# Output gates and a SiLU computed from tanh in a fused mLSTM, SiLU and Mish kernel

## The chip, the cores and the metric

One Trainium2 chip, one of its cores. The metric is device time in microseconds of one execution of the whole program; lower is better. Three runs of the kernel before took 449.8 to 451.85 us, with a median of 450.71 us.

## What is computed

Three stages in float32, each fed by the one before. Batch 2, 8 heads, 768 positions, head dimension 40; the two feed-forward layers have a model width of 320 and a hidden width of 2048, on 1536 tokens.

```python
# attention (mLSTM), per position t
m_new = max(f + m, i);  f_stab = exp(f + m - m_new);  i_stab = exp(i - m_new)
C = f_stab * C + i_stab * outer(v, k);  n = f_stab * n + i_stab * k
y = sigmoid(o_gate) * (C @ q) / max(abs(n @ q), 1)
# layer one
h = x @ w_in;   g = h * sigmoid(h);            x = g @ w_out
# layer two
h = x @ w_in2;  g = h * tanh(softplus(h));     out = g @ w_out2
```

## The kernel before

**Tiles and stages.** The 768 positions are cut into six chunks of 128. The attention of a chunk is done in its parallel form: TensorE makes the scores (L748), ScalarE the decay weights as exponentials (L704 for the first two chunks, L730 for the others), VectorE multiplies them (L757, the tile `pt`), TensorE sums (L762), and the state carried from chunk to chunk is updated by L846, L853, L860 and L866. The output of a chunk is divided and gated (L805 to L819), where the tile `y` holds the output gate, and turned (L897, L907, L910) into `xh` and `xl`. The gate's sigmoid is line L649, once for each chunk, in place, on 128x640 elements.

**The feed-forward layers.** A float32 matrix product is made of three passes on split operands: a rounded high part and the remainder. The weights of a layer come as 16 tiles of 128x704. Each is loaded by a DMA into one of three `wr` buffers, put together by ScalarE (L471, L463) and VectorE (L477), and split into `wh` (ScalarE, L503; VectorE, L501) and `wl` (GpSimd, L497). Hidden units are processed in pairs of 128. For a pair, `gemm1` (L930) writes the PSUM tile `h`, an activation makes `g`, `parts` splits that into `gh` (GpSimd, L955) and `gl` (VectorE, L957), and `gemm2` (L947 to L949) adds to the PSUM tiles `o`. Layer one has 48 such pairs (8 pairs of units for each of 6 chunks), layer two as many. `gemm2` of a pair is issued two pairs behind its `gemm1`. PSUM holds two tiles `h`; `g` has two buffers. In layer one the activation is ScalarE's SiLU (L964); layer two uses ScalarE's Mish function (L973, L974).

**The first two chunks of layer one** are done in two halves: units 0 to 4 first and 5 to 7 later, since the weights are still coming. The first part's result is stored by L983 (ScalarE) and the second added by L987 (VectorE), both from PSUM into the tile `y`.

**ScalarE's tables.** A function of ScalarE is served from a table that must be loaded. In the kernel before, the exponential, the sigmoid, the SiLU and the Mish function are marked with four different tables ("exp", "sig", "silu", "mish"). A change of table is an instruction ACT_TABLE_LOAD ahead of the function; the profile gives it the function's line.

**The order of the work.** Nothing runs in the order in which it is written. Each piece is registered with an engine, a cost in us, its tiles and for some its table. A planner in the kernel then simulates the engines, and in its model a change of table costs 1.28 us and adds a penalty of 20 to an operation that needs one. It draws 1,500 random variations of the priorities from a fixed seed, and keeps the best order. This order is fixed when the program is built; each engine then works through its own list, and an instruction that waits holds up those behind it. Transfers are all issued by SyncE's queue.

Of the kernel before, what the change touches and what calls it, by code (L numbers as in the profile page):

```python
# [13 lines left out]
AF = mybir.ActivationFunctionType  # L14
ALU = mybir.AluOpType
# [23 lines left out]
class Plan:  # L39
# [13 lines left out]
    def buf(self, pool, shape, dtype, tag, bufs=1, name=None):  # L53
        b = Buf(pool, shape, dtype, tag, bufs, name or tag)
        ring = self.rings.setdefault((id(pool), tag), [])
        b.before = ring[-bufs] if len(ring) >= bufs else None
        b.prev = ring[-1] if ring else None
        ring.append(b)
        return b

    def op(self, eng, cost, fn, r=(), w=(), table=None, anchor=None, hurry=0.0, duty=1.0, spare=False, after=(), size=0.0, grain=0.0):
        o = Op()
        o.eng, o.cost, o.fn, o.table, o.anchor, o.hurry = eng, cost, fn, table, anchor, hurry
        o.n, o.duty, o.spare, o.size, o.grain = len(self.ops), duty, spare, size, grain
        deps, order = {}, {}

        def need(ops):
            for d in ops:
                deps[d.n] = d

        for write, keys in ((False, r), (True, w)):
            for k in keys:
                b, sub = k if isinstance(k, tuple) else (k, None)
                subs = [s for s in dict.fromkeys([*b.wr, *b.rd]) if sub is None or s is None or s == sub]
                for s in subs:
                    need(b.wr.get(s, ()))
                    if write:
                        need(b.rd.get(s, ()))
                if not b.users:
                    if b.before is not None:  # L80
                        need(b.before.users)
                    if b.prev is not None:
                        order[b.prev.users[0].n] = b.prev.users[0]
                else:
                    order[b.users[0].n] = b.users[0]
                b.users.append(o)
        for d in after:
            order[d.n] = d
        for k in r:
            b, sub = k if isinstance(k, tuple) else (k, None)  # L90
            b.rd.setdefault(sub, []).append(o)
        for k in w:
            b, sub = k if isinstance(k, tuple) else (k, None)
            if sub is None:
                b.wr, b.rd = {None: [o]}, {}
            else:
                b.wr[sub], b.rd[sub] = [o], []
        deps.pop(o.n, None)
        order.pop(o.n, None)
        o.deps = list(deps.values())  # L100

        o.order = [d for d in order.values() if d.n not in deps]
        self.ops.append(o)
        return o
# [265 lines left out]
def kernel(  # L370
# [17 lines left out]
    DM = out.shape[1]  # L388
# [10 lines left out]
    op, buf = plan.op, plan.buf  # L399
    pe, act, dve, pool = nc.tensor, nc.scalar, nc.vector, nc.gpsimd  # L400
# [242 lines left out]
    y1 = [buf(sb, [128, B, DM], F32, f"y{c}") for c in range(NCH)]  # L643
# [2 lines left out]
    last = NCH - 1  # L646

    def sigm(c, after):
        return op("ACT", 0.74, lambda: act.activation(out=y1[c].t, in_=y1[c].t, func=AF.Sigmoid),  # L649
           w=[y1[c]], table="sig", after=after)  # L650

    def load_o(c, after=()):
        dma(y1[c], None, lambda: y1[c].t, lambda: og[c], 128 * B * DM * 4, after=after)
# [1 line left out]
    def attention(c):  # L655
# [79 lines left out]
        for i in SIGS.get(c, ()):  # L735
            sigm(i, [last_e[0]])
# [217 lines left out]
    def parts(g, gh, gl):  # L954
        op("POOL", 0.63, lambda: pool.tensor_scalar(  # L955
            out=gh.t, in0=g.t, scalar1=1.0, scalar2=1.0, op0=ALU.mult, op1=ALU.mult), r=[g], w=[gh])
        op("DVE", 0.75, lambda: dve.tensor_tensor(  # L957
            out=gl.t, in0=g.t, in1=gh.t.bitcast(F32), op=ALU.subtract), r=[g, gh], w=[gl], grain=1.0)

    def silu(hp):  # L960
        g = buf(sb, [128, 512], F32, "g", bufs=2)
        gh = buf(sb, [128, 512], F32R, "gh", bufs=3)
        gl = buf(sb, [128, 512], F32R, "gl", bufs=3)
        op("ACT", 0.6, lambda: act.activation(out=g.t, in_=hp.t, func=AF.Silu), r=[hp], w=[g], table="silu")  # L964
        parts(g, gh, gl)
        return gh, gl

# [11 lines left out]
    def store_y(c, b, po, part):  # L979
        y = y1[c]  # L980

        def first():
            act.copy(out=y.t[:, b, :], in_=po.t[:, 0:DM])  # L983


        def more():
            dve.tensor_tensor(out=y.t[:, b, :], in0=y.t[:, b, :], in1=po.t[:, 0:DM], op=ALU.add)  # L987

        if part == 2:
            op("DVE", 0.49, more, r=[po], w=[(y, b)])  # L990
        else:
            op("ACT", 0.43, first, r=[po], w=[(y, b)])
# [21 lines left out]
    def block(l, c, ps_, part=0, lag=2):  # L1014
        po = None
        for p in ps_:
            hp = hidden(l, p)
            for f in range(2):
                gemm1(l, 2 * p + f, xt[l, c], hp)
            g = (silu, mish)[l](hp)  # L1020
            while len(pend) >= lag:
                drain()
            if po is None:
                po = [buf(ps, [128, 512], F32, f"o{b}") for b in range(2)]
            pend.append((l, c, p, g, po, p == ps_[0], p == ps_[-1], part))
# [7 lines left out]
    for c in range(YFIRST):  # L1033
        load_o(c)
    sig = [sigm(c, ()) for c in SIGS.get(-1, ())]
    dma(sel, None, lambda: sel.t, lambda: cst[0:16, NC0:], 16 * 126 * 4)
    if G1 == 0:
# [171 lines left out]
```

## Time and profile before

| | |
|---|---|
| median of three runs | 450.71 us (449.8 to 451.85) |
| span of the profiled execution, first to last instruction | 447.9 us |
| mean granted TensorE clock | 0.973 |
| busy share: TensorE / weight load | 97% / 95% |
| busy share: VectorE / ScalarE / GpSimd | 44% / 56% / 32% |

The whole time of the profiled execution is not listed apart from its span; the median of the runs lies 2.8 us above the span, and covers what lies ahead of the first and behind the last instruction. In the profile PE is TensorE, PEld its weight loads, ACT ScalarE, DVE VectorE, POOL GpSimd and SP SyncE; L964 is line 964 of the kernel. A busy share is a mean over stages that have different limits, so the rows below are taken by stage.

### The profile page before, as it was taken

To read this page: it belongs to the slowest core of one execution; us is meant where nothing else is said; L and a number is where in the kernel's file an instruction comes from. 1 tells how busy PE (TensorE), PEld (TensorE's weight loads), DVE (VectorE), ACT (ScalarE), POOL (GpSimd) and SP (SyncE) were. 2 spreads that over 40 slices of the span, in tenths; PEclk is the share of its full clock that TensorE was granted. 3 is DMA by queue.
4 is the path that set the end of the run, shared out by engine and by line. 5 is a ranking of instruction groups with operands and counts; after the bars stand their busy time and mean duration, and the time that the engine had idled before them with its cause. 6 is when DMAs were issued, how large, how long until landed. Compare 5 with 4: busy or idle time off the path is not lost.

```text
span 447.9 us, 8297 instructions
## 1 busy us (share of the span) xinstructions
PE 435.0 (97%) x3366; PEld 424.6 (95%) x3366; DVE 196.2 (44%) x340; ACT 249.4 (56%) x441; POOL 145.1 (32%) x208
## 2 busy tenths in 40 slices
PE   7978989999999999999999999999999999999997
PEld 4858889999999999999999999999999999999996
DVE  4486587644774555664442644322131221221111
ACT  1898667799989888873124447433343333333331
POOL 1777686862361434122113996300000000000000
PEclk9956969999999999999999999999999999999999
DMA  7869979152475767865000453100000000000000
GB/s 223 301 225 268 324 241 318 67 166 71 112 249 185 291 213 277 279 205 201 3 1 1 131 156 103 34 31 0 2 31 0 1 31 0 31 1 0 31 2 29
DMA packets 16785, 54.18 MB, mean 121 GB/s; under 512 B 2003, under 2 KB 3731, under 8 KB 16267
## 3 DMA queue, kind: packets, MB, share of 16 engines
q1 hardware_dynamic: 16747, 53.65, 36.5%
q8 instruction: 26, 0.43, 0.4%
q14 instruction: 12, 0.10, 0.1%
HBM read 45.88 MB, written 7.77 MB: 120 GB/s over the span
## 4 chain that ended last, share of the span: by engine, by line
PE 89%; POOL 4%; ACT 3%; DMA 2%; issue 1%; DVE 1%; POOLq 0%; ACTq 0%
PE h L930 29%; PE o L947 12%; PE o L949 12%; PE o L948 12%; PE s L930 10%; PE a L762 4%; PE s L748 2%; POOL wl L497 2%; PE a L897 2%; DMA wr<-w 2%; PE o L445 1%; PE a L781 1%; PE a L846 1%; ACT e L704 1%; PE h L694 1%
## 5 line engine op out<-in xcount | busy, mean ns | idle before, releaser
L947 PE MATMUL o<-wh,gh 128*128 128x320 f32 x384 | 121.1, 315 | 0.0
L949 PE MATMUL o<-wh,gl 128*128 128x320 f32 x384 | 119.1, 310 | 0.4 <-DVE gl L957 0.4
L948 PE MATMUL o<-wl,gh 128*128 128x320 f32 x384 | 118.4, 308 | 0.0
L930 PE MATMUL h<-xh,wh 128*128 128x256 f32 x432 | 111.0, 286 | 0.0
L930 PE MATMUL h<-xl,wh 128*128 128x256 f32 x432 | 109.0, 281 | 0.0
L975 DVE TENSOR_TENSOR gl<-e,gh 128x512 fp32r<-128x512 f32 x48 | 33.8, 703 | 126.6 <-ACT e L974 126.6
L930 PEld LDWEIGHTS h<-xh,wh 128*128 128x128 f32 x432 | 82.5, 191 | 0.6 <-issue 0.2
L930 PEld LDWEIGHTS h<-xl,wh 128*128 128x128 f32 x432 | 82.3, 190 | 0.0
L949 PEld LDWEIGHTS o<-wh,gl 128*128 128x128 f32 x384 | 72.1, 188 | 0.7 <-DVE gl L957 0.7
L947 PEld LDWEIGHTS o<-wh,gh 128*128 128x128 f32 x384 | 72.3, 188 | 0.5
L948 PEld LDWEIGHTS o<-wl,gh 128*128 128x128 f32 x384 | 72.3, 188 | 0.0
L497 POOL TENSOR_TENSOR wl<-wt,wh 128x192 fp32r<-128x192 f32 x96 | 64.7, 704 | 15.9 <-ACT wh L503 13.4
L957 DVE TENSOR_TENSOR gl<-g,gh 128x512 fp32r<-128x512 f32 x48 | 40.6, 851 | 43.9 <-POOL gh L955 43.7
L930 PE MATMUL h<-xh,wl 128*128 128x256 f32 x288 | 58.0, 283 | 0.0
L955 POOL TENSOR_SCALAR gh<-g 128x512 fp32r<-128x512 f32 x48 | 32.3, 674 | 77.2 <-ACT g L964 74.9
L964 ACT ACTIVATE g<-h 128x512 f32<-128x512 f32 x48 | 28.5, 598 | 41.4 <-PE h L930 40.9
L930 PEld LDWEIGHTS h<-xh,wl 128*128 128x128 f32 x288 | 44.3, 190 | 0.0
L973 ACT ACTIVATE gh<-h 128x512 fp32r<-128x512 f32 x24 | 14.5, 602 | 50.5 <-PE h L930 50.4
L973 ACT ACTIVATE gh<-s 128x512 fp32r<-128x512 f32 x24 | 14.4, 601 | 49.5 <-PE s L930 49.5
L930 PE MATMUL s<-xh,wh 128*128 128x256 f32 x144 | 36.4, 282 | 0.0
L930 PE MATMUL s<-xl,wh 128*128 128x256 f32 x144 | 36.0, 279 | 0.0
L477 DVE SCALAR_TENSOR_TENSOR wt<-wt,wr 128x704 int32<-128x704 int32 x32 | 31.8, 997 | 5.7 <-ACT wt L463 5.1
(101 smaller groups left out, 621.0 us busy)
## 6 DMA issues: line engine op xcount, KB each, us to landing
wr<-w SPq DMA_DIRECT2D x32, 704.0 KB, 6.4
wd<-wt SPq DMA_DIRECT2D x16, 352.0 KB, 5.3
wt<-wd SPq DMA_DIRECT2D x16, 352.0 KB, 3.1
vk<-vk SPq DMA_DIRECT2D x6, 729.0 KB, 4.0
kq<-qk SPq DMA_DIRECT2D x12, 320.0 KB
e<-gd SPq DMA_DIRECT2D x8, 256.0 KB, 5.9
ga<-gd SPq DMA_DIRECT2D x8, 256.0 KB, 3.3
y<-og SPq DMA_DIRECT2D x6, 320.0 KB, 11.3
```

The lines of the kernel that those rows point to most:

```text
L477: dve.scalar_tensor_tensor(out=ti, in0=ti, scalar=3, in1=r.t[:, :, 0], op0=ALU.logical_shift_left, op1=ALU.bitwise_or)
L497: pool.tensor_tensor(out=wl.t[:, k], in0=t.t[:, k], in1=wh.t[:, k].bitcast(F32), op=ALU.subtract)
L762: pe.matmul(out=pa.t[:, h * V:(h + 1) * V], lhsT=pt.t[:, i * 128:(i + 1) * 128], rhs=vb.t[:, b, h * V:(h + 1) * V], start=True, stop=True,)
L930: pe.matmul(out=hp.t[:, f % 2 * 256:(f % 2 + 1) * 256], lhsT=w.t[:, k], rhs=xx.t[:, i, :], start=(n == 0), stop=(n == len(terms) - 1),)
L947: pe.matmul(out=o, lhsT=gh.t[:, ts], rhs=wh.t[:, O], start=(first and f == 0), stop=False)
L948: pe.matmul(out=o, lhsT=gh.t[:, ts], rhs=wl.t[:, O], start=False, stop=False)
L949: pe.matmul(out=o, lhsT=gl.t[:, ts], rhs=wh.t[:, O], start=False, stop=(end and f == 1))
L955: op("POOL", 0.63, lambda: pool.tensor_scalar(out=gh.t, in0=g.t, scalar1=1.0, scalar2=1.0, op0=ALU.mult, op1=ALU.mult), r=[g], w=[gh])
L957: op("DVE", 0.75, lambda: dve.tensor_tensor(out=gl.t, in0=g.t, in1=gh.t.bitcast(F32), op=ALU.subtract), r=[g, gh], w=[gl], grain=1.0)
L964: op("ACT", 0.6, lambda: act.activation(out=g.t, in_=hp.t, func=AF.Silu), r=[hp], w=[g], table="silu")
L973: op("ACT", 0.6, lambda: act.activation(out=gh.t, in_=hp.t, func=AF.Mish), r=[hp], w=[gh], table="mish")
L975: op("DVE", 0.7, lambda: dve.tensor_tensor(out=gl.t, in0=g.t, in1=gh.t.bitcast(F32), op=ALU.subtract), r=[g, gh], w=[gl])
```

## The change

The sigmoid of the output gates becomes `0.5 * tanh(x / 2) + 0.5`: ScalarE makes the tanh in place, GpSimd multiplies and adds in place. Layer one's SiLU becomes `(tanh(h / 2) + 1) * h`, which is twice the SiLU: ScalarE makes the tanh from PSUM, and a new VectorE instruction adds one and multiplies by `h`, again from PSUM. The factor two is taken out where the layer's result leaves PSUM: ScalarE's copy becomes a multiplication by 0.5, and VectorE's addition takes a scalar 0.5 with it. All three functions are now marked with the exponential's table; Mish keeps its own. The planner gets 54 more operations (6 on GpSimd, 48 on VectorE) and other tables, and plans the whole order anew.

```diff
     def sigm(c, after):
-        return op("ACT", 0.74, lambda: act.activation(out=y1[c].t, in_=y1[c].t, func=AF.Sigmoid),
-           w=[y1[c]], table="sig", after=after)
+        o = op("ACT", 0.74, lambda: act.activation(out=y1[c].t, in_=y1[c].t, func=AF.Tanh, scale=0.5),
+           w=[y1[c]], table="exp", after=after)
+        op("POOL", 0.85, lambda: pool.tensor_scalar(
+            out=y1[c].t, in0=y1[c].t, scalar1=0.5, scalar2=0.5, op0=ALU.mult, op1=ALU.add), w=[y1[c]])
+        return o
...
-        op("ACT", 0.6, lambda: act.activation(out=g.t, in_=hp.t, func=AF.Silu), r=[hp], w=[g], table="silu")
+        op("ACT", 0.6, lambda: act.activation(out=g.t, in_=hp.t, func=AF.Tanh, scale=0.5), r=[hp], w=[g], table="exp")
+        op("DVE", 0.7, lambda: dve.scalar_tensor_tensor(
+            out=g.t, in0=g.t, scalar=1.0, in1=hp.t, op0=ALU.add, op1=ALU.mult), r=[hp], w=[g])
         parts(g, gh, gl)
...
         def first():
-            act.copy(out=y.t[:, b, :], in_=po.t[:, 0:DM])
+            act.mul(out=y.t[:, b, :], in_=po.t[:, 0:DM], mul=0.5)
...
         def more():
-            dve.tensor_tensor(out=y.t[:, b, :], in0=y.t[:, b, :], in1=po.t[:, 0:DM], op=ALU.add)
+            dve.scalar_tensor_tensor(
+                out=y.t[:, b, :], in0=po.t[:, 0:DM], scalar=0.5, in1=y.t[:, b, :], op0=ALU.mult, op1=ALU.add
+            )
```

## Rows read from the trace of the kernel before

**Rows 1.** Head of the page.

```profile
span 447.9 us, 8297 instructions
```

**Rows 2.** Windows by stage: length, busy us (instructions) by engine, granted clock, DMA share, GB/s.

```profile
0.00:70.00 70.00, 60.35 (x409) 52.40 (x409) 45.01 (x90) 48.18 (x91) 45.65 (x68) 0.83 0.82 265
...
120.00:130.00 10.00, 10.00 (x91) 9.68 (x90) 8.70 (x13) 8.30 (x12) 6.24 (x7) 1.00 0.62 188
130.00:266.00 136.00, 136.00 (x1101) 134.68 (x1101) 69.49 (x120) 81.41 (x133) 50.99 (x73) 1.00 0.49 167
266.00:448.00 182.00, 178.69 (x1377) 178.37 (x1376) 44.21 (x73) 67.07 (x127) 13.59 (x22) 1.00 0.07 24
```

**Rows 3.** Windows within the first 70 us; engines in order PE, PEld, DVE, ACT, POOL.

```profile
20.00:23.00 3.00, 2.76 (x25) 2.65 (x23) 0.42 (x1) 2.99 (x7) 2.81 (x7) 1.00 0.57 163
23.00:26.00 3.00, 0.77 (x4) 0.77 (x4) 2.31 (x4) 3.00 (x6) 0.53 (x2) 0.66 0.22 33
...
45.00:50.00 5.00, 4.57 (x33) 4.31 (x32) 3.23 (x5) 3.62 (x6) 2.85 (x4) 1.00 1.03 287
...
57.00:62.00 5.00, 5.00 (x36) 4.73 (x35) 4.32 (x9) 2.99 (x5) 4.31 (x6) 0.61 0.70 252
62.00:67.00 5.00, 3.98 (x23) 3.79 (x22) 3.78 (x10) 3.01 (x5) 4.24 (x7) 0.71 0.69 191
```

**Rows 4.** Chain that ended last, 0 to 75 us: start us, us, what.

```profile
17.73 1.28 ACT L649
...
19.77 1.28 ACT L704
...
23.69 0.04 DVE wt L477
...
24.50 0.69 DVE pt L757
...
46.94 0.90 DVE wt L477
...
47.85 7.42 DMA wr<-w
```

**Rows 5.** The same chain later, two pairs of layer one.

```profile
131.99 1.89 PE h L930 x16
135.63 1.89 PE h L930 x16
```

**Rows 6.** ScalarE's timeline near 40 us: start, us, instruction.

```profile
39.63 1.28 ACT L649 ACT_TABLE_LOAD   x1
...
41.68 1.28 ACT L964 ACT_TABLE_LOAD   x1
42.97 0.60 ACT L964 ACTIVATE g<-h 128x512 f32<-128x512 f32 x1
```

**Rows 7.** Groups by line, whole span: busy us, mean ns of one | idle before, releaser.

```profile
L964 ACT ACTIVATE g<-h 128x512 f32<-128x512 f32 x48 | 28.5, 598 | 41.4 <-PE h L930 40.9
...
L964 ACT ACT_TABLE_LOAD x15 | 19.2, 1283 | 3.4 <-PE h L930 3.2
...
L649 ACT ACT_TABLE_LOAD x6 | 7.7, 1283 | 0.1
L957 DVE TENSOR_TENSOR gl<-g,gh 128x512 fp32r<-128x512 f32 x48 | 40.6, 851 | 43.9 <-POOL gh L955 43.7
L757 DVE TENSOR_TENSOR pt<-e,s 128x512 f32<-128x512 f32 x16 | 10.7, 682 | 4.9 <-PE s L748 4.9
L955 POOL TENSOR_SCALAR gh<-g 128x512 fp32r<-128x512 f32 x48 | 32.3, 674 | 77.2 <-ACT g L964 74.9
```

**Rows 8.** Waits of DVE, 70 to 266 us: us in total, times, longest.

```profile
DVE gl L957 <- POOL gh L955: 40.2, 28, 3.6
DVE nm L789 <- PE a L781: 11.6, 6, 3.1
```

**Rows 9.** Waits of SyncE's queue, 0 to 75 us.

```profile
SPq L403 <- DVE wt L477: 28.2, 13, 5.0
```

## The prediction, made before the changed kernel was built or run

> **What bounds the kernel now.** I read the windows first, cut by stage. From 130 us on TensorE is busy in all of the window, 136.00 of 136, at a granted clock of 1.00, and from 266 us to the end it misses only 3.3 us, which is the last store behind the last product [rows 2]. At 120 to 130 us the other engines are at their fullest (DVE 8.70 of 10, ACT 8.30) and TensorE still misses nothing. So behind the first 70 us the kernel is as long as its matrix products, and ScalarE's work and its table loads are no limit there. In the first 70 us it is otherwise: TensorE is idle for 70 - 60.35 = 9.65 us, and its mean granted clock is 0.83, so that part of what it does there goes at the lower of its two levels, 1.2 GHz [rows 2]. Only these 70 us can be made shorter. Removing 20 table loads or 50 from the rest is worth nothing by itself.
>
> Next I read where the holes of the first 70 us lie. From 20 to 26 us TensorE is busy for 2.76 + 0.77 of 6 us, a hole of 2.47 us; DMA falls to a share of 0.22 at the same place, and ScalarE is busy for 5.99 of the 6 us [rows 3]. The chain of waits says why: it runs through ScalarE from 17.73 us, a table load, the sigmoid, a second load to come back to the exponential, exponentials, the two steps of a weight tile, then VectorE's joining of that tile (23.69 us) and only behind it, in VectorE's fixed order, the `pt` that TensorE waits for (24.50 us) [rows 4]. The same joining frees a `wr` buffer, and SyncE's queue waits for such joins for 28.2 us in all [rows 9]; so the weight stream stands still there too. Later there are smaller holes: 0.43 us at 45 to 50 and 1.02 us at 62 to 67 us, with clocks of 0.61 and 0.71 from 57 to 67 us [rows 3].
>
> **The change, part by part.**
>
> *Table loads removed.* With one table for exponentials, gates and SiLU, the 15 loads in front of the SiLU and the 6 in front of the sigmoid go, 19.2 + 7.7 us of ScalarE at 1,283 ns each [rows 7], and so do those by which the exponential comes back. But only four of all of these lie in the first 70 us: two at 17.73 and 19.77 us [rows 4], and two at 39.63 and 41.68 us [rows 6].
>
> The first two are 2.56 us on the chain, with ScalarE full around them. What they delay is the hole of 2.47 us, so TensorE can win between 0 (if `pt`'s buffers or another engine become the last to be ready) and 2.47 us. I take the whole of it, because the chain between the loads and `pt` has nothing in it but ScalarE and one VectorE join, and because the weight stream, which is let go by the same join, moves with it. Term one: -2.47 us.
>
> Of the second two, the load at 41.68 us delays the first SiLU to 42.97 us [rows 6]. That starts the path to the first `gl`, for which TensorE misses 0.43 us [rows 3]. The SiLU gains 1.28 us, or 2.56 with the other load, and loses the new VectorE instruction (below, 0.68 us). The join at 46.94 us, which the chain goes through into a transfer of 7.42 us [rows 4], could come earlier too, but the DMA engines show a share of 1.03 there [rows 3], so an earlier issue only queues. Between 0 and -2.56 us, I take the small hole. Term two: -0.4 us.
>
> How much one switch costs decides both terms. The trace has a load at 41.68 us that takes 1.28 us, and the SiLU behind it starts at 42.97 us, 0.01 us after it ends [rows 6]. The Trainium skill, ScalarE: Activation LUTs, "What ACT_TABLE_LOAD costs", adds a drain of about 1.38 us to the load, 2.66 us for a switch. By that the first two switches would hold up the weight stream by 5.3 us instead of 2.56, and if TensorE followed the stream the forecast would be an estimated 445.0 us. The trace shows no room for such a drain behind the load, so 1.28 us stands.
>
> *The new VectorE instruction* reads `g` and PSUM and writes 128x512 elements, 48 times. The nearest row is `pt`, which has the same shape and also one operand in PSUM: 682 ns; the other end is `gl` with 851 ns while GpSimd works [rows 7]. I take 0.68 us, 48 x 0.68 = 33 us. The first follow the SiLU at 42.97 us [rows 6], where VectorE has room (busy 3.23 of 5 us at 45 to 50) [rows 3]; the rest falls in the stretch where VectorE is about half busy, 69.49 of 136 us [rows 2]. It lies in the path of each pair and also keeps `h` longer. Two pairs follow each other at 135.63 - 131.99 = 3.64 us, of which one pair's `gemm1` is 1.89 [rows 5]. A tile `h` is needed again two pairs later, so 2 x 3.64 - 1.89 = 5.4 us after it is complete. ScalarE's 0.60 and VectorE's 0.68 leave 4.1 us of slack. `gemm2`, two pairs behind, has still more: its path needs 0.60 + 0.68 + 0.67 + 0.85 = 2.8 us against 2 x 3.64 = 7.3 us from the end of its `gemm1` to its turn (two `gemm1` and two `gemm2`). Term three: 0, between 0 and what the rival below gives.
>
> *The new GpSimd instruction*, 128x640, 6 times: `gh` with 512 columns takes 674 ns [rows 7], so 0.84 us by columns, 5.1 us in all. Two gates fall before 70 us [rows 4, 6]. GpSimd works for 45.65 us of these 70 [rows 2], so each could cost from 0 to 0.84 us. But it is busy for only 0.53 of 3 us at 23 to 26 and 2.85 of 5 at 45 to 50 us [rows 3], and the first two chunks' gates leave time to choose. I take 0, with 1.7 us for the range.
>
> *tanh for SiLU and sigmoid, multiply for copy, scalar-tensor-tensor for add*: same engines, shapes and number of instructions. I take 0. The SiLU's 598 ns and the store's time may differ by a few ns, in a stretch that TensorE covers. No DMA is added.
>
> *The order.* The planner draws anew, with 54 more operations and no price on changing between exponentials, gates and SiLU. What it finds in the first 70 us I can't work out. The trace bounds it by the idle 9.65 us on the one side; I allow 2 us either way.
>
> **The sum.** 447.9 [rows 1] - 2.47 - 0.4 = 445.0 us of span. The median of the runs lies 2.8 us above the profiled span, so 447.8 us. About 0.5%, 2.25 us, is what a measurement can tell from no change: faster is below 448.5, slower above 453.0.
>
> **The rivals.**
>
> *The start gets tighter all over (B).* Freed of the switching penalty, exponentials of the third chunk and SiLU can alternate, and feed TensorE in the holes at 57 to 67 us: 1.02 us of idleness and, at clocks of 0.61 and 0.71, 0.39 x 5 + 0.29 x 5 = 3.4 us of lower rate, of which I count half. 447.8 - 1.0 - 1.7 = 445.1 us. For it speaks that both are there to be had; against it, that GpSimd is busy for 4.31 and 4.24 of 5 us there [rows 3] and gains nothing.
>
> *Hidden behind the weight stream (C).* The hole at 20 to 26 us goes, but the weight tiles come no earlier, because the DMA engines are full at 45 to 50 us, and TensorE waits later for the 2.47 us that it won: 447.8 + 2.5 = 450.3 us. For it speaks the share of 1.03 [rows 3]. Against it: the stream stood nearly still at 23 to 26 us (0.22), so time given there isn't lost to a full queue.
>
> *VectorE's list blocks (D), slower.* The new instruction stands in a list in which `nm` and `gl` wait for others for up to 3.1 and 3.6 us [rows 8], and at 120 to 130 us VectorE is busy 8.70 of 10 us. Where such a wait and the work queued behind it exceed the 4.1 us of slack of `h`, TensorE stalls, which it never does now. Eight attention halves lie behind 70 us; a microsecond lost at each is +8, with the gain 447.8 + 8 = 455.8 us. It decides once the stalls exceed 453.0 - 447.8 = 5.2 us in sum. Against it: the planner models VectorE's occupation and these waits, and a single wait stays below the slack.
>
> *The loads don't go (E).* If tanh were served from another table than the exponential, every switch would stay, and only VectorE's and GpSimd's work be added: 451 to 453 us. The trace has no tanh. The Trainium skill, ScalarE: Activation LUTs, "Table sets: the hidden batching unit", lists tanh in the exponential's set; no run here shows it yet.
>
> **How the numbers follow.** The forecast (A) gets 0.46, with a range of its own from 446.3 to 449.3; B 0.15, C 0.21, D 0.15, E 0.03. Faster: 0.38 of A and all of B, 0.53. Same: 0.08 of A, 0.17 of C, 0.02 of E, 0.27. Slower: D, 0.04 of C and 0.01 of E, 0.20. The range reaches 2 us below B for a luckier order, 443, and up to 453.5, which takes in C with both GpSimd terms (450.3 + 1.7) and leaves most of D out.
>
> **What would show it.** Right: only two or three table loads in the whole trace; the chain between 17 and 25 us without L649's load; TensorE's hole at 20 to 26 us gone or below 1 us; the idle time of the first 70 us down from 9.65 to about 7 us; behind it TensorE as full as now, and L964's new VectorE instruction near 0.68 us. Wrong: idle time of TensorE behind 70 us with VectorE as its releaser (D); a new hole between 45 and 70 us as large as the old one (C); or a hole that the new order opened elsewhere in the start.

## The result, and the profile after

The changed kernel takes 455.09 us (median of 4 runs, 452.82 to 458.7) where the kernel before takes 450.25 us on the same chip: a ratio of 1.0119, 95% interval 1.0075 to 1.0164. The forecast was 447.8 us, and the measured time lies above the range. By the prediction's own bound (453.0 us) this is "slower", to which it gave a chance of 0.20.

Head of the page, windows by stage (columns as in [rows 2]) and groups by line of the changed kernel:

```profile
span 454.1 us, 8366 instructions
```

```profile
0.00:70.00 70.00, 57.08 (x372) 47.63 (x373) 48.02 (x87) 38.89 (x80) 42.45 (x64) 0.85 0.77 239
...
120.00:130.00 10.00, 10.00 (x84) 9.47 (x83) 8.59 (x18) 6.75 (x16) 5.40 (x7) 1.00 0.77 243
130.00:266.00 136.00, 136.00 (x1102) 134.69 (x1101) 87.09 (x149) 55.02 (x102) 49.73 (x70) 1.00 0.50 161
```

```profile
L968 DVE SCALAR_TENSOR_TENSOR g<-g,h 128x512 f32<-128x512 f32 x48 | 32.9, 685 | 26.7 <-ACT g L967 26.4
...
L651 POOL TENSOR_SCALAR y<-y 128x640 f32<-128x640 f32 x6 | 4.6, 763 | 9.8 <-ACT y L649 9.8
...
L607 ACT ACT_TABLE_LOAD x1 | 1.3, 1283 | 0.8 <-PEq L1206 0.8
L978 ACT ACT_TABLE_LOAD x1 | 1.3, 1283 | 0.0
```

The span grew by 6.2 us over [rows 1]. Table loads: two are left, one at the start and one before Mish; all others are gone, as the Trainium skill, ScalarE: Activation LUTs, "Table sets: the hidden batching unit", has it with tanh in the exponential's set. The new VectorE instruction takes 685 ns. Behind 70 us TensorE is as full as in [rows 2], though VectorE now works 87.09 of 136 us there instead of 69.49. The visible loss lies in the first 70 us: TensorE is busy for 57.08 us instead of 60.35, so it misses 12.92 us instead of 9.65.

Windows within the start, changed kernel:

```profile
15.00:20.00 5.00, 4.88 (x28) 4.03 (x29) 1.83 (x6) 1.32 (x6) 0.00 (x0) 0.55 0.82 314
20.00:23.00 3.00, 3.00 (x20) 2.72 (x21) 1.15 (x5) 2.14 (x7) 0.55 (x1) 0.61 0.12 35
23.00:26.00 3.00, 3.00 (x33) 2.80 (x30) 0.42 (x1) 1.84 (x8) 1.40 (x2) 1.00 0.32 76
45.00:50.00 5.00, 4.75 (x37) 4.48 (x36) 4.18 (x6) 1.72 (x3) 5.00 (x8) 1.00 0.99 292
57.00:62.00 5.00, 4.71 (x42) 4.59 (x42) 3.96 (x9) 3.38 (x6) 2.57 (x5) 1.00 0.84 249
62.00:67.00 5.00, 2.52 (x21) 2.32 (x21) 4.87 (x7) 2.51 (x5) 5.00 (x8) 0.97 0.89 249
```

One of these windows in the kernel before:

```profile
15.00:20.00 5.00, 5.00 (x49) 4.62 (x49) 3.21 (x7) 4.50 (x12) 3.63 (x3) 1.00 0.82 268
```

Against [rows 3]: the hole at 20 to 26 us is closed (6.00 of 6 us busy). But the clock, which was 1.00 at 15 to 23 us before, is 0.55 and 0.61 there, and at 62 to 67 us TensorE now misses 2.48 us instead of 1.02 (it waits at L849 for VectorE's `nm`, L792). What happens just ahead of the low clock is seen on three engines. VectorE's timeline of the changed kernel (start, us, instruction):

```profile
8.21 1.28 DVE L538 TENSOR_TENSOR_SCAN ga<-ga 80x512 f32<-80x512 f32 x1
9.52 1.39 DVE L576 TENSOR_SCALAR ga<-ga,gc 16x128 f32<-16x128 f32 x1
10.95 1.37 DVE L565 TENSOR_TENSOR ga<-ga 80x128 f32<-80x128 f32 x1
...
13.84 1.22 DVE L576 TENSOR_SCALAR ga<-ga,gc 16x128 f32<-16x128 f32 x1
```

GpSimd's timeline and then TensorE's, same kernel:

```profile
9.57 1.26 POOL L546 TENSOR_TENSOR ga<-ga 80x512 f32<-80x512 f32 x1 [6.90 <-DVE ga L538]
10.91 1.26 POOL L551 TENSOR_TENSOR ga<-ga 80x512 f32<-80x512 f32 x1
...
13.73 1.26 POOL L565 TENSOR_TENSOR ga<-ga 80x512 f32<-80x512 f32 x1
```

```profile
15.12 0.29 PE L600 MATMUL a<-ct,ga 80*128 80x80 f32 x1 [1.67 <-DMA qq<-q]
```

VectorE's timeline of the kernel before, the same stretch:

```profile
7.79 0.29 DVE L565 TENSOR_TENSOR ga<-ga 80x128 f32<-80x128 f32 x1
8.09 0.28 DVE L576 TENSOR_SCALAR ga<-ga,gc 16x128 f32<-16x128 f32 x1
...
9.45 0.28 DVE L576 TENSOR_SCALAR ga<-ga,gc 16x128 f32<-16x128 f32 x1
10.73 1.28 DVE L538 TENSOR_TENSOR_SCAN ga<-ga 80x512 f32<-80x512 f32 x1
```

The gate arithmetic of the first chunks comes in two lots: chunks 0 and 1 (two tiles of 80x128) and chunks 2 to 5 (80x512). Before, the scan over the second lot (L538, 80x512) stood behind the last gate operation of the first. In the new list it stands ahead of the last of them. When it ends, GpSimd starts its own 80x512 operations on the second lot, and three of VectorE's small operations beside them take 1.39, 1.37 and 1.22 us instead of 0.28 or 0.29. Each of the three ends within 0.2 us of the end of the GpSimd instruction beside it. The last one ends at 15.06 us, and TensorE, which needs its `ga` for L600, stands from 13.45 to 15.12 us. (The releaser in brackets, `qq`, is not the one that came last: L600 reads `ga`.) Then the clock falls.

### The profile page after: what moved, and what is told of

It is laid out like the page before. It is cut to its first block, busy times and chain, and to the rows that moved or that the text cites. A ratio compares the mean times of both kernels' runs of the same rounds, so it can differ in the third digit from the quotient of the medians.

```text
span 454.1 us, 8366 instructions
## 1 busy us (share of the span) xinstructions
PE 437.9 (96%) x3366; PEld 425.1 (94%) x3366; DVE 230.8 (51%) x388; ACT 209.1 (46%) x409; POOL 149.7 (33%) x214
## 4 chain that ended last, share of the span: by engine, by line
PE 81%; POOL 6%; DVE 5%; DMA 4%; issue 2%; ACT 1%; SPq 1%; POOLq 0%; ACTq 0%
PE h L933 26%; PE o L950 11%; PE o L952 11%; PE o L951 11%; PE s L933 10%; PE a L765 3%; PE s L751 3%; POOL wl L497 3%; DMA qq<-q 2%; DMA e<-gd 2%; PE a L900 2%; POOL gh L958 1%; PE a L784 1%; PE a L849 1%; DVE wt L477 1%
## 5 line engine op out<-in xcount | busy, mean ns | idle before, releaser
L933 PE MATMUL h<-xl,wh 128*128 128x256 f32 x432 | 110.2, 283 | 0.0
L968 DVE SCALAR_TENSOR_TENSOR g<-g,h 128x512 f32<-128x512 f32 x48 | 32.9, 685 | 26.7 <-ACT g L967 26.4
```

The source lines that it names most:

```text
L933: pe.matmul(out=hp.t[:, f % 2 * 256:(f % 2 + 1) * 256], lhsT=w.t[:, k], rhs=xx.t[:, i, :], start=(n == 0), stop=(n == len(terms) - 1),)
L968: op("DVE", 0.7, lambda: dve.scalar_tensor_tensor(out=g.t, in0=g.t, scalar=1.0, in1=hp.t, op0=ALU.add, op1=ALU.mult), r=[hp], w=[g])
```

## The experiments

A list is the order in which the planner's operations are issued. In the runs on lists the search is left out and a written-out list is used, so that a single instruction can be moved. Each median is compared with the kernel before on the same chip; the ratios can be compared between rows, the medians only within a chip. "Tanh alone" and the two runs with a part of the new instructions (e5, e9, e10, e12) leave out what the output needs and serve to time the rest.

| run | us | ratio (95% interval) |
|---|---|---|
| e1 changed instructions, list of before | 457.53 | 1.0168 (1.0116 to 1.0220) |
| e2 instructions of before, new list | 470.85 | 1.0456 (1.0394 to 1.0517) |
| e5 tanh alone, list of before | 449.56 | 0.9997 (0.9970 to 1.0024) |
| e9 tanh and GpSimd's six, list of before | 449.08 | 0.9987 (0.9967 to 1.0006) |
| e10 tanh and VectorE's 48, list of before | 455.06 | 1.0119 (1.0083 to 1.0154) |
| e6, e7 before, seeds 2 and 4 | 449.02, 450.78 | 0.9998 (0.9969 to 1.0027), 1.0034 (1.0007 to 1.0061) |
| e8, e4 changed, seeds 2 and 3 | 451.11, 450.83 | 1.0035 (1.0015 to 1.0055), 1.0023 (1.0001 to 1.0046) |
| e3 changed, scan moved | 452.61 | 1.0065 (1.0034 to 1.0097) |
| e13 and cut moved | 450.44 | 1.0008 (0.9990 to 1.0025) |
| e14 and gate transfers later | 449.96 | 0.9999 (0.9985 to 1.0013) |
| e17 and tiles placed as before | 448.17 | 0.9969 (0.9952 to 0.9986) |
| e16 before, scan ahead | 451.17 | 1.0035 (1.0013 to 1.0056) |
| e18 before, tiles placed as after | 452.03 | 1.0046 (1.0022 to 1.0069) |
| e11 before, gate transfers later | 448.13 | 0.9966 (0.9938 to 0.9994) |
| e12 tanh alone, gate transfers later | 448.24 | 0.9964 (0.9936 to 0.9993) |
| e15 changed, seed 3, gate transfers later | 450.16 | 1.0020 (1.0001 to 1.0039) |

### List and instructions apart (e1, e2)

```diff
-        for o in best:
-            o.fn()
+        for n in ORDER:      # e1: before's list, the 54 new operations put in where due
+            self.ops[n].fn() # e2: kernel before, the new list without those 54
```

> The changed kernel's instructions in the order that the kernel before runs in; the 54 new instructions are put in where their inputs are due, nothing is planned anew. Theory T (the newly drawn order is slower, the new instructions are not): 446 to 450 us, at or below the kernel before's 450, no table loads but two, and TensorE's idle time in the first 70 us at or below 9.65 us. Rival R (the VectorE and GpSimd instructions themselves cost 5 us, in any order): 453 us or more.

> The kernel before's instructions (sigmoid and SiLU functions, with their table loads) in the order that the changed kernel runs in; the 54 new ones are left out, nothing is planned anew. T: as slow as the changed kernel or slower, 453 to 460 us, since the order carries the loss and the loads come on top. R: about 450 us, since what costs is left out.

Measured: 457.53 and 470.85 us. Neither list carries the other's instructions, and the forecast of e1 that the old list would be 446 to 450 us with them fell; e2 lies above both of its forecasts too. In e2 the trace has 31 table loads, in a list that was drawn without a price on them. In e1 the start keeps its gain: the step that stood at 23.69 us in [rows 4] comes at 22.05 us. But gemm1 of the first pair starts at 38.49 us, as before at 38.38, and behind 70 us, where the planned lists show no hole, TensorE now waits for the new instructions. So e1 had to be taken apart.

### Loads, gate arithmetic and products one at a time (e5, e9, e10)

```diff
-        act.activation(out=y1[c].t, in_=y1[c].t, func=AF.Sigmoid)   # and Silu
+        act.activation(out=y1[c].t, in_=y1[c].t, func=AF.Tanh, scale=0.5)
...
+        pool.tensor_scalar(...)           # e9 alone
+        dve.scalar_tensor_tensor(...)     # e10 alone
```

> The order of the kernel before, tanh in place of sigmoid and SiLU, and none of the 54 new instructions: the output lacks the halving and adding behind the gates and the product behind the tanh. It shows what the table loads alone are worth in that order. Theory T (the loads do hold up the start, by the 2.9 us of the prediction): 446 to 448 us, with the first 70 us idle for 7 us or less. Rival L (the loads were covered by other engines, and their time is lost again at the next wait): 449 to 451 us, like the kernel before.

> The order of the kernel before, tanh in place of sigmoid and SiLU, with the 6 new GpSimd instructions for the gates and without the 48 VectorE products (so layer one's activation is tanh alone). It parts the 7 us that the 54 new instructions cost in that order. Theory V (VectorE's products in a list that was not made for them are what costs): 449 to 451 us. Rival G (GpSimd's six in front of the weight splits): 455 us or more.

> The same order, with the 48 VectorE products and without the 6 GpSimd instructions (so the gates are tanh alone). V: 455 to 458 us, TensorE idle behind 70 us with VectorE's product or what follows it as the releaser. G: 449 to 451 us.

Measured: the missing loads are worth nothing (0.9997), the six GpSimd instructions cost nothing (0.9987), and VectorE's 48 cost about 5.5 us over e5 in a list that was not drawn for them (1.0119 against 0.9997). TensorE's timeline in e10, with what ended its idle time in brackets:

```profile
86.55 0.38 PE L870 MATMUL h<-xh,wh 128*128 128x256 f32 x1 [1.29 <-DVE g L905]
95.64 0.41 PE L887 MATMUL o<-wh,gh 128*128 128x320 f32 x1 [1.54 <-POOL gh L895]
96.75 0.42 PE L889 MATMUL o<-wh,gl 128*128 128x320 f32 x1 [0.55 <-DVE gl L897]
```

This is rival D as it was described: gemm1 waits for a tile `h` that the product (L905) still reads, and gemm2 for the parts of `g`.

Where the gain of the loads goes is read in e5. Its windows, then the same windows of the kernel before:

```profile
20.00:23.00 3.00, 2.71 (x26) 2.59 (x24) 2.10 (x4) 3.00 (x7) 2.92 (x6) 1.00 0.67 171
23.00:26.00 3.00, 2.30 (x24) 2.13 (x25) 2.37 (x5) 3.00 (x9) 3.00 (x4) 1.00 0.97 293
...
54.00:66.00 12.00, 12.00 (x64) 11.70 (x64) 8.23 (x17) 6.34 (x11) 8.63 (x13) 0.50 0.61 204
```

```profile
54.00:66.00 12.00, 11.53 (x79) 10.98 (x77) 8.68 (x18) 7.17 (x12) 10.30 (x16) 0.72 0.76 254
```

The hole at 20 to 26 us shrinks from 2.47 to 0.99 us, the transfers go on through it (share 0.97 instead of 0.22 at 23 to 26 us), and the first gemm1 starts at 36.62 us instead of 38.38. VectorE's join, which stood at 23.69 us in [rows 4], is at 20.91 us:

```profile
20.91 0.89 DVE L416 SCALAR_TENSOR_TENSOR wt<-wt,wr 128x704 int32<-128x704 int32 x1 [0.90 <-ACT wt L402]
```

Then, in the chain of waits of e5 and in its TensorE timeline, and below them the same step of the kernel before:

```profile
40.91 11.56 DMA vk<-vk
...
52.51 1.10 PE a L702 x8
```

```profile
52.51 1.10 PE L702 MATMUL a<-vk,pt 128*128 128x41 f32 x8 [1.25 <-DMA vk<-vk]
```

```profile
53.59 1.08 PE L762 MATMUL a<-vk,pt 128*128 128x41 f32 x8 [0.56 <-DMA vk<-vk]
```

The keys and values of a chunk take 11.56 us on full DMA engines (share 1.02 at 40 to 50 us), and land at 52.47 us. In the kernel before they are issued at 42.40 us and land at 53.55, after 11.15 us. So the queue takes back 0.4 of the 1.5 us by which they are issued earlier, and TensorE still starts on them 1.1 us earlier. But it waits 1.25 us for them instead of 0.56, and from 54 us on runs at 0.50 instead of 0.72 until 66 us. It ends the same work on chunk 1 (L702, L762) at 63.45 us, in the kernel before at 62.56: 2.0 us are lost in this stretch, in which e5's timeline shows no wait of TensorE. The transposition of chunk 1 starts at 68.08 us, in the kernel before at 67.19: all that was won is given back, most of it at the lower clock.

### Other draws of the list (e6, e7, e8, e4)

```diff
-SEED = 1
+SEED = 2    # e6 before, e8 changed; 4 in e7 (before), 3 in e4 (changed)
```

> The kernel before with the planner's seed 2 in place of 1: the same work in another order. It shows how much an order drawn anew moves the time without any change. Theory T (orders differ by several us on the chip): between 447 and 456 us, not necessarily at 450. Rival (orders are worth the same, and what the change added is what cost): 449 to 451 us.

> The kernel before with seed 4. As with seed 2: T 447 to 456 us, the rival 449 to 451 us.

> The changed kernel with seed 2. T: an order without the scan of chunks 2 to 5 in front of chunk 1's gates, so below the 455 us of seed 1, 447 to 453 us. Rival (the new instructions cost whatever the order): about 455 us.

> The changed kernel with another seed of the planner's random search (3 instead of 1): the same work, another order drawn from the same rules. T: the loss was a property of one draw; this order has the scan of chunks 2 to 5 behind chunk 1's gates, so 446 to 451 us. R: about 455 us, since the work is the same.

Measured: redrawing the list of the kernel before moves it by 1.8 us (449.0 to 450.8). Two other lists of the changed kernel give 451.1 and 450.8 us, so about 4 of the 4.8 us belong to the list of seed 1 (0.84% and 0.96% by the ratios, each with an uncertainty of 0.5%). 1.0 to 1.6 us are left in these by the ratios; part of that is the tiles' places, below.

### Two instructions of the list (e3, e13, e16)

```diff
 VectorE's list, e3 and e13 (e16: the opposite move in the kernel before)
-  scan over chunks 2 to 5, ahead of chunk 1's last gate operations
   chunk 1's last gate operations
+  scan over chunks 2 to 5
 GpSimd's list, e13
-  second mask cut of 128x512 (waits for its transfer)
   gh of the pair
+  second mask cut
```

> The changed kernel in its own order but for one VectorE instruction: the scan of the gates of chunks 2 to 5 goes behind the last gate instruction of chunk 1, so that GpSimd's gate instructions start later. T, narrowed to this place (T1: GpSimd's instructions stretch VectorE's gate instructions, 1.39 us instead of 0.28, and TensorE waits and falls to its lower clock): the stretched instructions are back near 0.3 us, TensorE's hole at 13.5 to 15.1 us is gone, 449 to 452 us. R: unchanged, about 455 us. If the loss sits in several places of the new order: 452 to 454 us.

> The kernel with the scan moved (452.6 us, 0.65% over the kernel before), and one more instruction of its list moved: on GpSimd the second mask cut of 128x512, which waited 2.69 us for its transfer at 46.1 us with the high part of a gate tile behind it, goes behind that high part. Theory P (the order: a gate tile of the first gemm stood behind a cut that waited for a transfer): the high part runs at about 47 us instead of 49.4, TensorE's wait of 2.3 us for it at 47.7 to 50.05 is gone, and since TensorE did not stand there its clock stays at full speed behind 50 us (0.54 and 0.50 between 50 and 65 us before); 450.0 to 450.8, about 2 us less. Theory F (the transfers are full there, and TensorE would only wait for the next thing that they bring): the wait moves to the keys or to the weights behind 50 us, 452 to 453.

> The kernel before, its own list, and one instruction moved: VectorE's scan of the gates of chunks 2 to 5 goes ahead of the last gate operations of chunk 1, where the changed kernel has it. Theory S (that place costs, whatever the gates are computed from): the gate operations behind it take 1.2 to 1.4 us instead of about 0.28 beside GpSimd's 80x512 operations, TensorE stands some 1.5 us at 13 to 15 us, and the kernel is 2 to 3 us slower, 452 to 453 with the kernel before at 450. Theory N (it only cost with the other changes of the list): 449.5 to 450.5.

The mask cut is GpSimd's select on the tile `e` (L659), for which a transfer of `gd` must have landed.

Measured: 2.5 us from the scan and 2.2 more from the cut by the medians. By the ratios the scan is 0.54%, with an uncertainty as large (0.55%), and the cut 0.57% (uncertainty 0.36%); the two together, 1.11% (0.48%), are clear of noise. With both moved the changed kernel is level with the one before (1.0008). In e3 the small gate operations are back at 0.28 us, the clock is 1.00 at 15 to 25 us, and the first gemm1 starts at 35.60 us, in the changed kernel at 41.03. The next place is then seen on GpSimd and TensorE:

```profile
48.77 0.64 POOL L659 TENSOR_SCALAR_AFFINE_SELECT e<-e 128x512 f32<-128x512 f32 x1 [2.69 <-DMA e<-gd]
49.37 0.62 POOL L897 TENSOR_SCALAR gh<-g 128x512 fp32r<-128x512 f32 x1
```

```profile
50.05 0.41 PE L889 MATMUL o<-wh,gh 128*128 128x320 f32 x1 [2.32 <-POOL gh L897]
```

```profile
45.00:50.00 5.00, 2.73 (x21) 2.46 (x19) 1.26 (x2) 2.05 (x3) 2.31 (x4) 1.00 1.00 344
50.00:55.00 5.00, 4.36 (x17) 4.02 (x18) 2.00 (x2) 2.28 (x3) 2.76 (x5) 0.54 0.78 257
```

GpSimd stands 2.69 us for the cut's transfer with a `gh` queued behind it, TensorE stands for that `gh`, and its clock falls to 0.54. In the changed kernel itself TensorE waited only 0.55 us for the same `gh`:

```profile
53.74 0.42 PE L950 MATMUL o<-wh,gh 128*128 128x320 f32 x1 [0.55 <-POOL gh L958]
```

So the place of the cut shows its price once the scan no longer holds up what comes before it. In e13 the `gh` goes first, and the wait is 0.4 us in all:

```profile
47.75 0.62 POOL L897 TENSOR_SCALAR gh<-g 128x512 fp32r<-128x512 f32 x1 [1.30 <-DVE g L907]
48.60 0.99 POOL L659 TENSOR_SCALAR_AFFINE_SELECT e<-e 128x512 f32<-128x512 f32 x1 [0.23 <-DMA e<-gd]
```

In e16 the scan alone, put ahead in the kernel before, costs 1.6 us by the ratio (0.6 to 2.5 us; 1.1 by the medians), less than the 2 to 3 us expected. The stretching comes with it in part: the first L515 takes 1.23 us, the last one, on which TensorE waits, only 0.53. So TensorE stands for 0.47 us there and not for 1.67, and its clock at 15 to 20 us stays at 1.00. VectorE's and then TensorE's timeline of e16:

```profile
7.72 1.28 DVE L477 TENSOR_TENSOR_SCAN ga<-ga 80x512 f32<-80x512 f32 x1
...
9.20 1.23 DVE L515 TENSOR_SCALAR ga<-ga,gc 16x128 f32<-16x128 f32 x1
...
12.84 0.53 DVE L515 TENSOR_SCALAR ga<-ga,gc 16x128 f32<-16x128 f32 x1
```

```profile
13.43 0.29 PE L539 MATMUL a<-ct,ga 80*128 80x80 f32 x1 [0.47 <-DVE ga L515]
```

### The gates' transfers later (e11, e12, e14, e15)

```diff
 SyncE's queue
-  y of chunks 2 to 5, between the weight tiles from 29 us on
   weight tiles
+  y of chunks 2 to 5, behind the 15th weight tile (issued at 69 us in e11)
```

> The kernel before with four transfers moved in SyncE's queue, the gates of chunks 2 to 5 behind the 15th weight tile; all else in its order. They are not due before 100 us, and 1.3 MB leave the stretch in which the DMA engines are full. Theory C (the full DMA engines hold up the start): 447 to 449 us. Rival (they don't): 449.5 to 451 us.

> The same four transfers moved, with tanh alone in the same order (no table loads, none of the 54 new instructions; the output lacks what they do). C: without the full DMA engines the time of the table loads shows, 1 to 2.5 us below the kernel before with the transfers moved, 445 to 447.5 us. Rival (the loads' time is lost elsewhere too): the same as that kernel, within 0.7 us.

> The same, and the four transfers of the output gates of chunks 2 to 5 moved in SyncE's queue behind the fifteenth tile of weights (to some 75 us; first used at 100 us). In the kernel before this alone gave 1.5 us (448.1 against 449.7). Theory P: the same 1 to 2 us on top of the run beside it, 448.5 to 450. Theory F (the rest of the loss is the full transfers): the larger part of the loss goes here, 3 us or more below the run beside it, 448 to 450 as well, so what tells them apart is which of these two runs takes the step.

> The changed kernel with the list of seed 3 (450.8 us, 0.23% over the kernel before), in which the high part of that gate tile already stands ahead of the cut, and the same four transfers moved back. Theory F: what keeps the change from its gain is the full transfers at 36 to 60 us: 448.0 to 449.5, at least as fast as the kernel before with the same edit (448.1). Theory P (an order drawn by the planner is good or bad for reasons of its own): the same as without the edit, 450 to 451.

Measured: the kernel before gains 1.5 us (448.13), the changed one 0.1 to 0.4 us by the ratios (e15 against e4, e14 against e13), which is within the uncertainty; e14's forecast of 1 to 2 us was missed. In e12 the keys no longer hold TensorE, and still the missing loads give nothing over e11. TensorE's timeline of e12:

```profile
64.19 0.44 PE L837 MATMUL a<-ct,x 128*128 128x128 f32 x2 [3.13 <-DVE st L793]
```

TensorE finishes chunk 1's attention at the full clock by 61.06 us and then waits 3.13 us for its output, which comes through ScalarE's and GpSimd's splitting of a weight tile and GpSimd's gating of `y`. In e11 it gets there at 64.93 us, later by 0.74, without a wait. Behind the wait e12's clock is 0.72 from 64 to 70 us, e11's 0.96, and the next gemm2 starts at 68.78 us in e12 and at 68.33 in e11. So by the traces the wait for the keys is one of the two things that the loads' gain runs into, and the work of GpSimd and VectorE on chunk 1 is the other; behind both stands TensorE's lower clock. No run took the second away.

### The places of the tiles (e17, e18)

A tile gets its place in memory when it is first used, so a new list also moves the tiles.

```diff
+        first = {tag: ring[0] for (_, tag), ring in self.rings.items()}
+        for tag in PLACES:       # e17: order of first use in the kernel before
+            first[tag].t         # e18: kernel before, order of the changed one
         for n in ORDER:
             self.ops[n].fn()
```

> The changed kernel with the scan, the cut and the four gate transfers moved (449.96 us, ratio 0.9999), in the same order of instructions; only the places of its tiles in memory are those of the kernel before. A tile gets its place when it is first used, so a new order of the work gave the tiles other places. Behind 300 us, where TensorE never stands in either kernel, the weight loads of gemm1 take 190 ns in every list drawn for the change and 188 in every list drawn for the kernel before, whichever instructions are in the list, and 20 tiles s of layer two follow each other in 141.52 us instead of 140.91. Theory M (the places set this): the loads take 188 ns again, 20 tiles s take 140.9 us, and over 96 pairs 1.5 us are won: 448.3 to 448.8. Theory L (it is the list itself, which work runs beside which): 190 ns, 141.5 us and 450 us as without the edit.

> The other way round: the kernel before, its own order of instructions, the places of the tiles those of the changed kernel. Theory M: gemm1's weight loads take 190 ns, 20 tiles s take 141.5 us, and the kernel is 1.5 us slower, 451.5 with the kernel before at 450.0. Theory L: 188 ns, 140.9 us and 450.0.

Measured: 448.17 us with the edit, 449.96 without (0.9969 against 0.9999, on two chips); the other way round 452.03 us against 449.29. Groups by line of 300 to 430 us, one row each of the kernel before, the changed one, e17 and e18:

```profile
L930 PEld LDWEIGHTS h<-xh,wh 128*128 128x128 f32 x108 | 20.3, 188 | 0.0
```

```profile
L933 PEld LDWEIGHTS h<-xh,wh 128*128 128x128 f32 x102 | 19.4, 190 | 0.0
```

```profile
L875 PEld LDWEIGHTS h<-xh,wh 128*128 128x128 f32 x103 | 19.4, 188 | 0.0
```

```profile
L872 PEld LDWEIGHTS h<-xh,wh 128*128 128x128 f32 x108 | 20.5, 190 | 0.0
```

The weight load of gemm1 takes 188 ns with one set of places and 190 with the other, whatever the list and the instructions. TensorE is full in both, so the windows don't show it; the pace does. In e17, the first matmul of the 20th tile `s` from the end and of the last:

```profile
294.97 0.36 PE L875 MATMUL s<-xh,wh 128*128 128x256 f32 x1
...
435.88 0.28 PE L875 MATMUL s<-xh,wh 128*128 128x256 f32 x1
```

and in e18:

```profile
297.77 0.36 PE L872 MATMUL s<-xh,wh 128*128 128x256 f32 x1
...
439.29 0.27 PE L872 MATMUL s<-xh,wh 128*128 128x256 f32 x1
```

That is 140.91 us against 141.52 for 19 steps of two pairs each; 0.61 / 38 x 96 pairs = 1.5 us over the kernel. Which tile's place does it was not tried. The traces of the other seeds show the same two values: 188 ns in all three lists drawn for the kernel before (`before`, e6, e7), 190 in all three drawn for the changed one (`after`, e8, e4). So this part of the loss came with the change in each draw that was made, and not with seed 1 alone.

## Why the prediction was wrong

**Term one failed.** The step "I take the whole of it, because the chain [...] has nothing in it but ScalarE and one VectorE join, and because the weight stream [...] moves with it" held up to 37 us only, and in part: the stream moves, the join comes 2.78 us earlier, the hole shrinks to 0.99 us, gemm1 comes 1.76 us earlier (e5). The end doesn't move: 0.9997, so between -1.4 and +1.1 us, where -2.47 was summed. The time is taken back at 41 to 66 us: 0.4 us by a transfer that takes longer when it is issued earlier, and 2.0 us between the landing and the end of chunk 1's sums, where TensorE, having stood for 1.25 us, runs at the lower clock. This comes near rival C, whose 450.3 us e5 nearly met with 449.56, but C's mechanism was only a part: the tiles did come 1.1 us earlier. The argument against C ("time given there isn't lost to a full queue") looked at the queue where the hole was, and not where the tiles land, and neither it nor C counted the clock behind a new wait. With the queue relieved (e12) the gain was lost to chunk 1's gating. What the loads are worth in a list drawn for tanh alone was not tried.

**Term two** was not measured by itself; the hole of 0.43 us at 45 to 50 us is one of 0.25 us in the changed kernel. A drain behind each load, by which the forecast was 445.0 us, is not borne out: with the first two loads gone the join comes 2.78 us earlier, near the 2.56 us of the loads themselves and not 5.3.

**Term three was right for a list that is drawn for it, and for no other.** The price was 0.68 us, measured 685 ns; behind 70 us TensorE stands nowhere. In the old list the same instructions cost 5.5 us (e10), by the mechanism of D. D's time, 455.8 us, came close to the measured 455.09, but not by D: nothing was lost to waits behind 70 us.

**GpSimd's six instructions** cost 0 as forecast (e9), at 763 ns each in the changed kernel and 876 in e9, about the 0.84 us. **E fell**: two loads are left. **B's** higher clock at 57 to 67 us came (1.00 and 0.97), but with 2.77 us of idleness there instead of 1.02, in a kernel that was late by then.

**The order was the step that decided it.** "I allow 2 us either way" was too small; of the signs of being wrong, the last one came, a hole elsewhere in the start (13.45 to 15.12 us). The list of seed 1 costs, by the ratios of e3, e13 and the changed kernel, 0.54% (2.4 us) for the place of one scan and 0.57% (2.6 us) for the place of one cut, in the order in which they were moved; the scan's share alone is not clear of noise, the two together are. The places of the tiles, which no step thought of, cost 0.30% (1.35 us) by e14 and e17, and 0.46% (2.1 us) by e18. The first three sum to 6.4 us (2.4, 2.6 and 1.35), more than the 5.4 us of the ratio 1.0119; with 0.4 us for the gates' transfers that is what brings e17 below the kernel before. (They are steps of one row of runs and add up by that; what each is worth alone in the changed kernel was not tried.) "Behind the first 70 us the kernel is as long as its matrix products" was read from a busy share; the products themselves became 0.43% longer at the same share.

With all four moves, e17 runs at 448.17 us, faster than both kernels (0.9969). But the kernel before with only the gate transfers moved, e11, is as fast (0.9966, 448.13 us). So beside that kernel the change is worth nothing that these runs can tell, though e17's list had two moves by hand that e11's did not get; its loss was the list and the places that came with it.

One term of the sum was also read wrong, which decided nothing here: the 2.8 us between span and time. In every later run the profiled execution takes 1.7 to 1.8 us more than its span (here 455.81 against 454.1); by that the rest is that the profiled execution of the kernel before was quicker than the median.

What stays open: whether the scan costs more in the changed kernel (2.4 us) than in the kernel before (1.6), since the uncertainty covers the difference; what in the places slows the weight loads; and how much of the gain lost in e12 is GpSimd's and how much VectorE's.

## What to carry to other kernels

When an edit makes a planner draw its order anew, the new order and the new places of the tiles are changes of their own: run the old instructions in a fixed list, other seeds, and fixed places, before the time is put down to the edit. A microsecond won early counts only if the last of the things that the next stage waits for moves too; follow the transfers and each engine's list up to where TensorE stays full. In a list that is fixed, look behind each instruction that waits for a transfer for what stands queued, and beside each long GpSimd instruction for short VectorE ones that something waits for.

## What the runs showed of the hardware

Beside GpSimd's 80x512 instructions of 1.26 us, three of VectorE's 80x128 and 16x128 ones took 1.22 to 1.39 us instead of 0.28 or 0.29, and ended with them. The Trainium skill, SBUF — State Buffer, "SBUF: two separate sides", says that VectorE and GpSimd share a pair of ports, and that when a VectorE instruction has two inputs in SBUF (or runs in a mode that uses two ports), whichever of it and a GpSimd instruction starts first holds the pair for its whole instruction. The ends of the three instructions above agree; the start of the first does not, which by the trace lies 0.05 us ahead of GpSimd's (9.52 and 9.57 us). Nor do two others: while GpSimd's L555 ran from 12.26 to 13.75 us, VectorE's scan L559 took 0.82 us instead of 0.42 and ended at 13.15, and L568 (80x128, two operands) took its usual 0.29 us from 13.18 us on.

A weight load of 128x128 took 188 or 190 ns depending on where the tiles lay, in every run of either set and whatever the list; no other cause for the two values was found. A transfer of the keys and values took 11.56 us when issued at 40.91 us into DMA engines at a share of 1.02 (e5), and 11.15 us when issued at 42.40 us at a share of 1.00 (kernel before). Stands of TensorE in the start were mostly followed by a lower granted clock: 1.67 us by 0.55 at 15 to 20 us in the changed kernel, 2.32 us by 0.54 at 50 to 55 us in e3. Not always: in e14 TensorE was busy for 2.77 of the 5 us from 55 to 60 us, and the clock stayed at 1.00 until 70 us; in e13 TensorE was busy for 4.71 of the 5 us from 50 to 55 us, and the clock was 0.50 in the 5 us behind them.
